# FFT filter and gated FFN: the first batch's loads as 128 rows, and the next batch's first x loads asked for earlier

## The chip, the cores and the metric

The kernel runs on one core of one Trainium2 chip. The metric is the device time of one execution in microseconds (us); the median of three runs is 1565.5 us (1564.04 to 1566.27).

## What is computed

For each of 8 batches, x (3136 positions by 256 channels) is filtered in the frequency domain along the positions, and the result goes through a feed-forward block with a gate:

```python
X = np.fft.rfft(x, axis=1)
y = np.fft.irfft(X * (filt_r + 1j * filt_i)[None], n=3136, axis=1)   # (8, 3136, 256)
h = np.maximum(y @ w_in, 0.0)                                        # 256 -> 1024
conv[s] = sum(conv_w[k] * h[s + k - 1] for k in range(3))            # zero outside the batch
out = (h * sigmoid(conv) @ w_out).astype(np.float32)                 # 1024 -> 256
```

## The kernel before

The transform of length 3136 is split as 112 x 28. A batch passes four kinds of matmul work, each in 14 pairs of columns (`NP = 14`): the first stage (112-point transforms with the tables `s1`), the second stage (28-point), a multiplication with the filter (`filt`), and the way back (third and fourth stage, the fourth with the tables `m2` or `m2g`). Its result is y, kept in SBUF as a high and a low part; the feed-forward block then reads y.

The program has an opening and a main loop. In the **opening** batch 0 is transformed alone, and nothing of the feed-forward block runs:

- Stage 1 (`first_loads`, `turned_stage` with the tile `rows`): seven pairs of loads, each one table chunk (`tab`, four columns of `s1`, 112 rows of 1792 bytes) and one chunk of x (`rows`, 112 rows of 4096 bytes). TensorE multiplies (matmuls on tile `rows`, L333), ScalarE copies the result into `at` (L385).
- Meanwhile VectorE and GpSimd turn weights from float64 words (`raw`, 512 KB for each half, loaded with 128 rows of 4096 bytes by `load_weights`; `conv_raw`, 24 KB) into float32 pairs. The generator `early` issues these steps, 35 VectorE instructions during stage 1 (L168 to L180).
- Stage 2 (the loop over `i`): TensorE transposes (L341) and multiplies by the second-stage table (L246); VectorE applies the filter in three instructions for each pair (`filt`, L261 to L263) and GpSimd adds (L264, tile `z`, three buffers); TensorE multiplies again (L333, tile `z`), ScalarE copies into `bt` (L404). Each pair needs one filter tile `f` (128 rows of 4096 bytes, four buffers, `load_filter`), asked for when VectorE has done the filter of four pairs before.
- In the same loop, at `i = 14` and `15`, TensorE does the first stage of the first two pairs of batch 1 (`AHEAD = 2`, tile `xa`, L242), stored to DRAM from ScalarE's queue. Behind each of the two stands, on TensorE, a third-stage multiplication of batch 0 that frees a `z` buffer.
- Stage 3: the way back (L343, L272), y's high part on ScalarE (L154) and low part on VectorE (L157), with further conversion steps of `early` between.

In the **main loop** the feed-forward of batch b runs with the transforms of batch b+1 between its matmuls, laid out by the table `plan`. It loads x for batch 1 as the tile `tin` (112 rows).

All loads named here are issued by SyncE's queue (SP), in one order, and the engines' orders are those of the code. A DMA issue on SP waits until the issue eight places before it has landed, because there are eight semaphores in rotation, and SP stands still for all that follows meanwhile.

Of the kernel before, what the change touches and what calls it, by code (L numbers as in the profile page):

```python
# [9 lines left out]
F32 = mybir.dt.float32  # L10
# [7 lines left out]
N1 = 112  # L18
N2 = 28
G = 28  # L20
D = 256
# [7 lines left out]
def _k1(g, s):  # L29
    return g + 1 + 28 * s  # L30


def _w(num, den):
    return np.exp(-2j * np.pi * (np.asarray(num) % den) / den)


def _dft_tables():

    n1, n2, c, a = np.arange(N1), np.arange(N2), np.arange(N2), np.arange(N1)
    n = 28 * a + c[:, None]
    s1 = np.zeros((N1, N2, 112))
    m2 = np.zeros((112, N2, N1))
    for g in range(G):
        for s in range(2):  # L50
            if g == G - 1 and s == 1:
                s1[:, :, 2 * 28 + g] = 1.0
                s1[:, :, 3 * 28 + g] = ((-1.0) ** n1)[:, None]
                m2[2 * 28 + g] = 1.0 / S
                m2[3 * 28 + g] = (-1.0) ** a / S
                continue
            k1 = _k1(g, s)
            w = _w(k1 * (28 * n1[:, None] + n2[None, :]), S)
            s1[:, :, 2 * s * 28 + g] = w.real
            s1[:, :, (2 * s + 1) * 28 + g] = w.imag  # L60
            w = np.conj(_w(k1 * n, S))
            m2[2 * s * 28 + g] = 2 * w.real / S
            m2[(2 * s + 1) * 28 + g] = -2 * w.imag / S

    def s3(special):
        m = np.zeros((2, 2, 28, N2, 4))
        for s in range(2):
            for j in range(28):
                if special and s == 1:
                    if j == 0:  # L70
                        m[0, s, 0, :, 2] = 1.0
                        m[1, s, 0, :, 2] = (-1.0) ** c
                    elif j < 14:
                        w = np.conj(_w(j * c, N2))
                        m[0, s, j, :, 2] = 2 * w.real
                        m[1, s, j, :, 2] = -2 * w.imag
                    else:
                        w = np.conj(_w((56 + 112 * (j - 14)) * c, S))
                        m[0, s, j, :, 3] = 2 * w.real
                        m[1, s, j, :, 3] = -2 * w.imag  # L80
                    continue
                k2, sg = (j, 1) if j < 14 else (41 - j, -1)
                w = np.conj(_w(k2 * c, N2))
                m[0, s, j, :, 2 * s] = w.real
                m[1, s, j, :, 2 * s] = -sg * w.imag
                m[0, s, j, :, 2 * s + 1] = w.imag
                m[1, s, j, :, 2 * s + 1] = sg * w.real
        m = m.reshape(2, 56, 112)
        return np.concatenate([m[0], np.zeros((8, 112)), m[1]])

    def s2(special):
        m = np.zeros((112, 2, 2, 28))
        for s in range(2):
            for j in range(28):
                if special and s == 1:
                    if j == 0:
                        m[n2 * 4 + 2, 0, s, 0] = 1.0
                        m[n2 * 4 + 2, 1, s, 0] = (-1.0) ** n2
                    else:
                        w = _w(n2 * j, N2) if j < 14 else _w(n2 * (56 + 112 * (j - 14)), S)  # L100
                        r = 2 if j < 14 else 3
                        m[n2 * 4 + r, 0, s, j] = w.real
                        m[n2 * 4 + r, 1, s, j] = w.imag
                    continue
                k2, sg = (j, 1) if j < 14 else (41 - j, -1)
                w = _w(n2 * k2, N2)
                m[n2 * 4 + 2 * s, 0, s, j] = w.real
                m[n2 * 4 + 2 * s + 1, 0, s, j] = -w.imag
                m[n2 * 4 + 2 * s, 1, s, j] = sg * w.imag
                m[n2 * 4 + 2 * s + 1, 1, s, j] = sg * w.real  # L110
        re, im, gap = m[:, 0].reshape(112, 56), m[:, 1].reshape(112, 56), np.zeros((112, 8))
        return np.concatenate([re, gap, im, -im, gap, re], 1)

    turned = m2.reshape(4, G, N2, N1).transpose(1, 0, 2, 3).reshape(112, N2, N1)
    return {"s1": s1, "s2": s2(False), "s2s": s2(True), "one": np.eye(128), "s3": s3(False), "s3s": s3(True), "m2": m2, "m2g": turned}


def _bins():
# [12 lines left out]
def tile_fft_filter_gated_ffn(  # L131
# [18 lines left out]
    nc = tc.nc  # L150
# [42 lines left out]
    a_in = [t[:].rearrange("n (r g) d -> (n r) g d", g=G) for t in a_dram]  # L193
    b_out = [t[:].rearrange("n (r g) d -> (n r) g d", g=G) for t in b_dram]
    b_in = [t[:].rearrange("n p d -> p n d") for t in b_dram]
    xv = [x[b].rearrange("(p n) d -> p n d", n=N2) for b in range(B)]

    wc = ctx.enter_context(tc.tile_pool(name="wc", bufs=1))
# [10 lines left out]
    turned = [wc.tile([120, 2, D], F32, name=f"v{k}") for k in range(2)]  # L209
# [15 lines left out]
    NP = 14  # L225

    def pair(q):
        return slice(2 * q, 2 * q + 2)

    def load_in(pool, kind, b, q, bufs, tag):  # L230
        r = pool.tile([112, 2, D], F32, name=tag, bufs=bufs)
        nc.sync.dma_start(out=r, in_={"1": xv, "2": a_in, "4": b_in}[kind][b][:, pair(q)])
        return r
# [46 lines left out]
    conv_raw = tp.tile([128, 1, 6 * NF], I32, name="conv_raw", bufs=1)  # L280

    def load_weights(k, pool):
        raws[k] = raw = pool.tile([128, 2, 1024], I32, name="raw", bufs=1 if pool is tp else 2)
        for part, w in enumerate((w_in, w_out)):
            nc.sync.dma_start(out=raw[:, part], in_=w[:, 1024 * k:1024 * k + 1024])
# [23 lines left out]
    with (  # L309
# [4 lines left out]
        fts, tabs, rows, zs, pss = {}, {}, {}, {}, {}  # L314
# [33 lines left out]
        with tc.tile_pool(name="sq", bufs=2) as sq:  # L348
            at = sq.tile([128, KT, N2, 112], F32, name="at", bufs=1)

            def table(kind, c):
                pool, src, n = {"1": (sq, s1, 4), "4": (sc, m2g, 3)}[kind]
                tabs[kind, c] = t = pool.tile([112, 4, 112], F32, name=f"tab{kind}", bufs=n)
                nc.sync.dma_start(out=t, in_=src[:, 4 * c:4 * c + 4])

            def tab(kind, q):
                return tabs[kind, q // 2][:, 2 * (q % 2):2 * (q % 2) + 2]
# [4 lines left out]

            def first_loads(c):
                table("1", c)
                rows["x", c] = r = sq.tile([112, 4, D], F32, name="rows", bufs=5)
                nc.sync.dma_start(out=r, in_=xv[0][:, 4 * c:4 * c + 4])
                if c == 0:
                    nc.sync.dma_start(out=conv_raw[:, 0], in_=conv_w)
                if c in (0, 3):
                    load_weights(c // 3, sc)  # L370
                if c == 4:
                    for dst, t in ((one_sb, one), (s2_sb, s2[:, 0:120]), (s2s_sb, s2s[:, 0:120]), (s3_sb, s3), (s3s_sb, s3s)):
                        nc.sync.dma_start(out=dst, in_=t)
# [16 lines left out]
            for i in range(NP + 4):  # L390
                if i < NP:
                    back = [at[:, k].rearrange("p n (r g) -> p (n r) g", g=G) for k in range(KT)]
                    rows["2", i] = turn_back(lambda j, k: back[k][:, :, 2 * i + j], sq, "ar")
                if 0 <= i - 1 < NP:
                    pss[i - 1] = ps = bank()
                    second(ps, i - 1, rows.pop(("2", i - 1)))
                if 0 <= i - NP < AHEAD:
                    ps = bank()
                    by_column(ps, tab("1", i - NP), rows.pop(("1", i - NP)))
                    store(tp, "1", 1, i - NP, ps, 3, "st", nc.scalar)  # L400
                if 0 <= i - 4 < NP:
                    q = i - 4
                    ps = turned_stage(zs.pop(q), [by_r[q == NP - 1 and j].rearrange("p r c -> p (r c)") for j in range(2)])
                    nc.scalar.activation(bt[:, :, pair(q)], ps, AF.Copy)  # L404
                if 0 <= i - 2 < NP:
                    zs[i - 2] = filt(pss.pop(i - 2), i - 2, fts.pop(i - 2))
                    if i + 2 < NP:
                        load_filter(i + 2)
                if i == NP - 3:
                    table("1", 0)  # L410
                    for q in range(AHEAD):
                        rows["1", q] = load_in(sq, "1", 1, q, 2, "xa")
                    for c in range(3):
                        table("4", c)
                    load_weights(3, tp)
                if i >= NP + 1:
                    steps(early, 3)
# [193 lines left out]
    def want_table(n):  # L611
        for op in tables[n:n + 1]:
            src = {"1": s1, "4": m2}[op[0]]
            got_table[op] = t = tp.tile([112, 2, 112], F32, name="tab", bufs=4)
            nc.sync.dma_start(out=t, in_=src[:, pair(op[2])])

    def want_filter(n):
        for op in filters[n:n + 1]:
# [133 lines left out]
```

## Time and profile before

| | |
|---|---|
| median of three runs | 1565.5 us |
| profiled execution, its own time | 1563.99 us |
| its span, first to last instruction | 1562.2 us |
| busy share of TensorE / VectorE / ScalarE / GpSimd | 98% / 76% / 73% / 53% |
| mean granted TensorE clock | 0.994 |
| chain that ended last: TensorE / DMA / ScalarE | 94% / 2% / 2% |

In the profile PE is TensorE's matmul part, PEld its weight loads, DVE VectorE, ACT ScalarE, POOL GpSimd and SP SyncE; DMA issues have the mark q behind the engine. A fp32 matmul of the program stands in the trace as two.

### The profile page before, as it was taken

The page shows a single profiled execution, that of the slowest core. Times are in us where ns is not written, and L with a number is a line of the kernel's source. Part 1 is how long each engine was busy: PE and PEld are TensorE (multiplying, and loading weights), DVE is VectorE, ACT ScalarE, POOL GpSimd, SP SyncE. Part 2 cuts the span into 40 slices and gives each one's busy share as a digit, 9 for nine tenths or more (in the row PEclk, how much of TensorE's full clock was granted, in tenths as well). Part 3 has the DMA queues.
Part 4 walks back from the last instruction along what each step waited for, and adds up shares of the span by engine and source line. Part 5 has one row for each costly group of instructions (what it writes and reads, how often), then busy time and mean ns, then how long its engine had stood idle before and what let it go on. Part 6 is the DMA issues. An engine that isn't in the chain of part 4 may idle for free.

```text
span 1562.2 us, 26445 instructions
## 1 busy us (share of the span) xinstructions
PE 1524.6 (98%) x9202; PEld 1295.2 (83%) x9202; DVE 1184.5 (76%) x1810; ACT 1144.8 (73%) x1973; POOL 828.5 (53%) x721
## 2 busy tenths in 40 slices
PE   6899999999999999999999999999999999999999
PEld 5777788877897789977898778987799878999998
DVE  6887776787677786778767777777867888777776
ACT  2486678866797668866688667976678667888886
POOL 4535446544474555744566444745457454664444
PEclk9999999999999999999999999999999999999999
DMA  9857764466436654465554655356542543300000
GB/s 261 260 164 202 208 180 138 138 196 192 145 91 200 193 156 142 120 198 179 153 150 129 198 178 162 109 161 208 169 143 86 160 150 96 114 28 15 28 28 30
DMA packets 158164, 228.74 MB, mean 146 GB/s; under 512 B 16432, under 2 KB 108960, under 8 KB 158032
## 3 DMA queue, kind: packets, MB, share of 16 engines
q1 hardware_dynamic: 157552, 226.60, 48.9%
q8 instruction: 73, 1.20, 0.3%
q14 instruction: 59, 0.48, 0.1%
q10 hardware_dynamic: 480, 0.46, 0.1%
HBM read 156.35 MB, written 70.65 MB: 145 GB/s over the span
## 4 chain that ended last, share of the span: by engine, by line
PE 94%; DMA 2%; ACT 2%; issue 1%; SPq 0%; DVE 0%; POOL 0%; ACTq 0%; POOLq 0%
PE ps_h L185 12%; PE ps_h L186 12%; PE ps_h L187 12%; PE po L528 11%; PE po L530 11%; PE po L529 11%; PE ps_t L246 10%; PE ps_t L272 6%; PE ps_t L242 5%; PE ps L333 1%; DMA rows<-in_x 1%; PE ps_t L249 1%; PE ps L246 1%; PE ps L341 1%; PE ps L272 1%
## 5 line engine op out<-in xcount | busy, mean ns | idle before, releaser
L496 DVE SCALAR_TENSOR_TENSOR t<-ps_h,cw,t 128x510 f32<-128x510 f32 (+1 forms) x800 | 588.1, 735 | 302.1 <-ACT t L492 298.9
L160 POOL TENSOR_TENSOR g<-t,g 128x510 fp32r<-128x510 f32 (+1 forms) x400 | 506.0, 1274 | 203.4 <-ACT g L154 191.7
L528 PE MATMUL po<-wo,g 128*128 128x256 f32 (+1 forms) x1576 | 439.9, 279 | 0.1
L530 PE MATMUL po<-wo,g 128*128 128x256 f32 (+1 forms) x1576 | 439.1, 279 | 0.0
L529 PE MATMUL po<-wo,g 128*128 128x256 f32 (+1 forms) x1576 | 438.9, 278 | 0.0
L487 ACT ACTIVATE ps_h<-ps_h 128x512 f32<-128x512 f32 (+1 forms) x400 | 234.8, 587 | 243.0 <-PE ps_h L187 241.5
L264 POOL TENSOR_TENSOR z<-z,v 120x512 f32<-120x512 f32 x112 | 144.6, 1291 | 389.5 <-DVE v L263 337.9
L492 ACT ACTIVATE t<-ps_h,cw 128x510 f32<-128x510 f32 (+1 forms) x400 | 272.6, 682 | 104.2 <-POOL g L160 71.6
L185 PE MATMUL ps_h<-y,wi 128*128 128x512 f32 (+1 forms) x688 | 333.3, 484 | 0.5 <-DVE y L157 0.5
L528 PEld LDWEIGHTS po<-wo,g 128*128 128x128 f32 (+1 forms) x1576 | 296.9, 188 | 17.4 <-ACT g L154 0.3
L529 PEld LDWEIGHTS po<-wo,g 128*128 128x128 f32 (+1 forms) x1576 | 296.1, 188 | 17.0
L530 PEld LDWEIGHTS po<-wo,g 128*128 128x128 f32 (+1 forms) x1576 | 296.4, 188 | 0.6 <-POOL g L160 0.5
L186 PE MATMUL ps_h<-y,wi 128*128 128x512 f32 (+1 forms) x688 | 270.1, 393 | 0.0
L187 PE MATMUL ps_h<-y,wi 128*128 128x512 f32 (+1 forms) x688 | 269.9, 392 | 0.0
L502 DVE TENSOR_TENSOR t<-ps_h,t 128x510 f32<-128x510 f32 (+1 forms) x400 | 268.3, 671 | 0.9 <-ACT t L499 0.8
L499 ACT ACTIVATE t<-t 128x510 f32<-128x510 f32 (+1 forms) x400 | 245.2, 613 | 1.6 <-DVE t L496 1.5
L154 ACT ACTIVATE g<-t 128x510 fp32r<-128x510 f32 (+1 forms) x400 | 245.0, 613 | 0.2 <-DVE t L502 0.2
L160 POOL TENSOR_TENSOR y<-z,y 128x448 fp32r<-128x448 f32 x98 | 138.5, 1423 | 93.9 <-ACT y L154 91.9
L185 PEld LDWEIGHTS ps_h<-y,wi 128*128 128x128 f32 x688 | 130.2, 189 | 44.2 <-issue 23.8
L186 PEld LDWEIGHTS ps_h<-y,wi 128*128 128x128 f32 x688 | 130.5, 190 | 41.4 <-issue 24.3
L187 PEld LDWEIGHTS ps_h<-y,wi 128*128 128x128 f32 x688 | 130.0, 189 | 30.3 <-POOL wi L160 0.2
L237 ACT ACTIVATE st<-ps_t 112x512 f32<-112x512 f32 x194 | 114.1, 591 | 11.3 <-PE ps_t L242 11.0
(91 smaller groups left out, 1616.0 us busy)
## 6 DMA issues: line engine op xcount, KB each, us to landing
filt<-in_filt SPq DMA_DIRECT2D x98, 512.0 KB
tin<-a_dram SPq DMA_DIRECT2D x98, 224.0 KB
b_dram<-st SPq DMA_DIRECT2D x98, 224.0 KB
tin<-b_dram SPq DMA_DIRECT2D x98, 224.0 KB
tin<-in_x SPq DMA_DIRECT2D x96, 224.0 KB
a_dram<-st SPq DMA_DIRECT2D x96, 224.0 KB
out<-ot SPq DMA_DIRECT2D x45, 256.0 KB
tab<-in_m SPq DMA_DIRECT2D x98, 98.0 KB
```

The source lines that it names most:

```text
L154: nc.scalar.activation(dst, src, AF.Copy)
L160: nc.gpsimd.tensor_tensor(out=dst, in0=src, in1=hi.bitcast(F32), op=ALU.subtract)
L185: nc.tensor.matmul(ps, lhsT=wh, rhs=rh, start=start, stop=False, **kw)
L186: nc.tensor.matmul(ps, lhsT=wh, rhs=rl, start=False, stop=False, **kw)
L187: nc.tensor.matmul(ps, lhsT=wl, rhs=rh, start=False, stop=stop, **kw)
L492: nc.scalar.activation(t, hs[u, f][:, 1:n + 1], AF.Copy, scale=cw[:, 1, f:f + 1])
L496: nc.vector.scalar_tensor_tensor(out=t, in0=h[:, k:place(u)[2] + k], scalar=cw[:, k, f:f + 1], in1=t, op0=ALU.mult, op1=ALU.add)
L499: nc.scalar.activation(ts[u, f], ts[u, f], AF.Sigmoid)
L502: nc.vector.tensor_mul(ts[u, f], hs.pop((u, f))[:, 1:place(u)[2] + 1], ts[u, f])
L528: nc.tensor.matmul(o, lhsT=gh[:, c:c + n], rhs=wo[0][:, f], start=first, stop=False, skip_group_check=True)
L529: nc.tensor.matmul(o, lhsT=gh[:, c:c + n], rhs=wo[1][:, f], start=False, stop=False, skip_group_check=True)
L530: nc.tensor.matmul(o, lhsT=gl[:, c:c + n], rhs=wo[0][:, f], start=False, stop=last, skip_group_check=True)
```

## The change

Three things. The first-stage tables get 16 rows of zeros, so that the table chunk and the chunk of x of each pair in stage 1 are loaded as 128 rows; the last 16 rows of x are the first ones of batch 1, and the computation reads rows 0 to 111. The load of `conv_raw` goes from ahead of the first weights to behind the second pair. The two `xa` loads and their table, asked for at `i = 11` before, are asked for at `i = 5`, and `xa` too is loaded as 128 rows.

```diff
+    tall = np.zeros((128, N2, 112))
+    tall[:N1] = s1
-    return {"s1": s1, ...
+    return {"s1": tall, ...
...
+    xt = x.rearrange("b (p n) d -> (b p) n d", n=N2)
...
             def table(kind, c):
                 pool, src, n = {"1": (sq, s1, 4), "4": (sc, m2g, 3)}[kind]
-                tabs[kind, c] = t = pool.tile([112, 4, 112], F32, name=f"tab{kind}", bufs=n)
+                t = pool.tile([src.shape[0], 4, 112], F32, name=f"tab{kind}", bufs=n)
                 nc.sync.dma_start(out=t, in_=src[:, 4 * c:4 * c + 4])
+                tabs[kind, c] = t[0:112]
...
             def first_loads(c):
                 table("1", c)
-                rows["x", c] = r = sq.tile([112, 4, D], F32, name="rows", bufs=5)
-                nc.sync.dma_start(out=r, in_=xv[0][:, 4 * c:4 * c + 4])
-                if c == 0:
-                    nc.sync.dma_start(out=conv_raw[:, 0], in_=conv_w)
+                r = sq.tile([128, 4, D], F32, name="rows", bufs=5)
+                nc.sync.dma_start(out=r, in_=xt[0:128, 4 * c:4 * c + 4])
+                rows["x", c] = r[0:112]
                 if c in (0, 3):
                     load_weights(c // 3, sc)
+                if c == 1:
+                    nc.sync.dma_start(out=conv_raw[:, 0], in_=conv_w)
...
-                if i == NP - 3:
+                if i == 5:
                     table("1", 0)
                     for q in range(AHEAD):
-                        rows["1", q] = load_in(sq, "1", 1, q, 2, "xa")
+                        r = sq.tile([128, 2, D], F32, name="xa", bufs=2)
+                        nc.sync.dma_start(out=r, in_=xt[N1:N1 + 128, pair(q)])
+                        rows["1", q] = r[0:112]
+                if i == NP - 3:
                     for c in range(3):
                         table("4", c)
```

Only SP's order changes. At the program's start it stood so before (`tab` with `in_s` is a table chunk, `rows` the chunk of x, `raw` the weights):

```order
L354 DMA tab_111<-in_s 112x448
L366 DMA rows<-in_x 112x1024
L368 DMA conv_raw<-in_conv_w 128x48
L285 DMA raw<-in_w_in 128x1024
L285 DMA raw<-in_w_out 128x1024
L354 DMA tab_119<-in_s 112x448
L366 DMA rows<-in_x 112x1024
```

And now:

```order
L357 DMA tab_111<-in_s 128x448
L370 DMA rows<-in_x 128x1024
L288 DMA raw<-in_w_in 128x1024
L288 DMA raw<-in_w_out 128x1024
L357 DMA tab_118<-in_s 128x448
L370 DMA rows<-in_x 128x1024
L375 DMA conv_raw<-in_conv_w 128x48
```

The pairs carry 128 rows, and the 24 KB of `conv_raw` stand three places later, behind the first weights and the second pair.

In stage 2, SP's order among the filter loads `f` was this before, with three of the main loop's x loads (`tin`) between them:

```order
L361 DMA f<-in_filt 128x1024 x4
L232 DMA tin<-in_x 112x512
L361 DMA f<-in_filt 128x1024 x2
L232 DMA tin<-in_x 112x512
L361 DMA f<-in_filt 128x1024 x2
L232 DMA tin<-in_x 112x512
L361 DMA f<-in_filt 128x1024 x2
L354 DMA tab_532<-in_s 112x448
L232 DMA xa<-in_x 112x512 x2
L354 DMA tab_538<-in_m2g 112x448
```

And now:

```order
L365 DMA f<-in_filt 128x1024 x4
L357 DMA tab_400<-in_s 128x448
L418 DMA xa<-in_x 128x512 x2
L365 DMA f<-in_filt 128x1024 x6
L357 DMA tab_538<-in_m2g 112x448
L357 DMA tab_540<-in_m2g 112x448
L357 DMA tab_542<-in_m2g 112x448
L288 DMA raw<-in_w_in 128x1024
L288 DMA raw<-in_w_out 128x1024
L235 DMA tin<-in_x 112x512 x5
```

`xa` and its table moved ahead of the last six filter loads; and the scheduler, which the code does not tell so, put all five early `tin` loads behind them, where three stood among the filter loads and two behind the last weights before.

More of the change, by code (lines that the diff above doesn't have):

```diff
@@ L114, in _dft_tables @@
     turned = m2.reshape(4, G, N2, N1).transpose(1, 0, 2, 3).reshape(112, N2, N1)
-    return {"s1": s1, "s2": s2(False), "s2s": s2(True), "one": np.eye(128), "s3": s3(False), "s3s": s3(True), "m2": m2, "m2g": turned}
+    tall = np.zeros((128, N2, 112))
+    tall[:N1] = s1
+    return {"s1": tall, "s2": s2(False), "s2s": s2(True), "one": np.eye(128), "s3": s3(False), "s3s": s3(True), "m2": m2, "m2g": turned}
 def _bins():
@@ L614, in want_table @@
             got_table[op] = t = tp.tile([112, 2, 112], F32, name="tab", bufs=4)
-            nc.sync.dma_start(out=t, in_=src[:, pair(op[2])])
+            nc.sync.dma_start(out=t, in_=src[0:112, pair(op[2])])
     def want_filter(n):
```

## Prediction

> **What bounds the kernel now.** I read the page first, then the chain that ended last cut to its first 100 us, then the waits, the order of time on SP, VectorE and ScalarE, and stretches. The page says that TensorE is the bound of the program as a whole:
>
> ```profile
> PE 1524.6 (98%) x9202; PEld 1295.2 (83%) x9202; DVE 1184.5 (76%) x1810; ACT 1144.8 (73%) x1973; POOL 828.5 (53%) x721
> ```
>
> The change touches none of TensorE's work, so it can act only where TensorE isn't the bound. The chain up to 100 us (start, length, what) shows where that is:
>
> ```profile
> 3.55 8.56 DMA rows<-in_x
> 12.12 11.45 DMA rows<-in_x
> 27.45 5.61 PE ps L333 x32
> 58.63 6.88 DMA xa<-in_x
> ...
> 96.31 0.99 DVE y L157
> ```
>
> Up to 23.6 us the chain is loads of x, and at 58.6 us it is the load of `xa`. The waits of the opening (us in total, times, longest) name who stands still for them:
>
> ```profile
> DVE em L168 <- DMA raw<-in_w_out: 9.9, 1, 9.9
> PE ps L333 <- DMA rows<-in_x: 11.9, 3, 5.5
> DVE z L261 <- PE ps L246: 3.4, 1, 3.4
> PE ps L242 <- DMA xa<-in_x: 4.2, 1, 4.2
> DVE z L261 <- PE ps L333: 5.1, 1, 5.1
> ```
>
> TensorE waits three times for x, VectorE once for the first weights. From about 97.4 us, when the first feed-forward matmul starts, every engine's work is the same in both programs and nothing in it depends on absolute time. So the gain is how much earlier the opening ends.
>
> **Who bounds the opening.** Busy time of VectorE, the third figure after the length, in its three parts (PE, PEld, DVE, ACT, POOL, clock, DMA share, GB/s):
>
> ```profile
> 9.86:32.80 22.94, 16.58 (x96) 16.22 (x96) 22.01 (x35) 5.99 (x11) 13.99 (x18) 0.85 1.04 279
> 36.22:64.27 28.05, 25.22 (x156) 18.84 (x154) 26.91 (x39) 12.20 (x22) 15.32 (x12) 1.00 0.83 242
> 69.38:97.44 28.06, 26.48 (x205) 24.71 (x204) 27.35 (x33) 23.12 (x35) 14.19 (x28) 0.95 0.35 99
> ```
>
> VectorE is busy for 22.0 of 22.9 us, 26.9 of 28.1 and 27.4 of 28.1. Between lie two gaps, 32.8 to 36.2 and 64.3 to 69.4. The opening is then a sum: first weights landed (9.86), 22.94 of conversion, a gap of 3.42, thirteen filter steps of 2.16 (28.05), a gap of 5.11, and 28.06 to the first matmul of the feed-forward.
>
> ```profile
> 9.86 0.43 DVE L168 TENSOR_SCALAR em<-raw 128x512 int32<-128x512 int32 x1 [9.86 <-DMA raw<-in_w_out]
> 32.05 0.75 DVE L180 SCALAR_TENSOR_TENSOR em<-raw,em 128x512 f32<-128x512 uint32 x1
> 36.22 0.69 DVE L261 TENSOR_TENSOR z<-ps,f 120x512 f32<-120x512 f32 x1 [3.42 <-PE ps L246]
> 62.11 0.69 DVE L261 TENSOR_TENSOR z<-ps,f 120x512 f32<-120x512 f32 x1
> 69.38 0.69 DVE L261 TENSOR_TENSOR z<-ps,f 120x512 f32<-120x512 f32 x1 [5.14 <-PE ps L333]
> ```
>
> The change can take from the first term and from the two gaps. The other three are instructions that it leaves as they are.
>
> **Part 1, 128 rows.** The rate of loads of different kinds, from stretches with the same columns:
>
> ```profile
> 10.00:13.00 3.00, 0.76 (x4) 0.79 (x4) 2.86 (x6) 0.00 (x0) 0.00 (x0) 1.00 1.06 257
> 20.00:23.00 3.00, 0.37 (x4) 0.19 (x2) 2.79 (x5) 0.60 (x2) 2.94 (x5) 1.00 1.06 223
> 31.00:36.00 5.00, 4.12 (x27) 3.27 (x27) 1.73 (x3) 2.72 (x5) 2.05 (x3) 0.98 1.01 401
> ```
>
> In all three the DMA engines are full (share 1.0). From 31 to 36 us only filter tiles and weights move, 128 rows of 4 KB: 401 GB/s. From 10 to 13 it is mostly table chunks and x with 112 rows: 257. That a chunk of x alone, also of 4 KB rows, is slow shows on SP, whose issue waits for the landing eight places before; the times are thus landings:
>
> ```profile
> 12.12 0.33 SPq L366 DMA_DIRECT2D rows<-in_x  x1
> 12.91 0.35 SPq L373 DMA_DIRECT2D one_sb<-in_one  x1
> 14.71 0.31 SPq L373 DMA_DIRECT2D s_sb<-in_s  x1
> 15.51 0.31 SPq L373 DMA_DIRECT2D s2s_sb<-in_s2s  x1
> 17.72 0.36 SPq L373 DMA_DIRECT2D s_sb<-in_s  x1
> 23.64 0.31 SPq L354 DMA_DIRECT2D tab<-in_s  x1
> ```
>
> 12.12 is the landing of the second x chunk, 12.91 of a table, 14.71 of x, 15.51 table, 17.72 x, 23.64 the fifth x. A chunk of x (459 KB) takes 1.80 and 2.21 us after its table, 255 and 208 GB/s; a table (201 KB) 0.8 us. From 12.12 to 23.64 three pairs of 660 KB and 1.05 MB of weights land; the weights at 401 GB/s are 2.6 us, which leaves 8.9, or 2.97 a pair.
>
> With 128 rows a pair is 754 KB. At 401 GB/s it takes 1.88 us, 1.09 less. If only x speeds up (524 KB, 1.31 us) and the table stays at 0.8 us for its first 112 rows (0.9 for 128), it takes 2.2, 0.76 less. The rows of 1.8 KB haven't been seen with 128, so I keep both ends and take 0.9. Six pairs lie ahead of the restart at 27.45, which waits for the sixth chunk: 4.6 to 6.5 us earlier, 5.4 taken. From there ScalarE's last copy of stage 1 ended 6.2 us later:
>
> ```profile
> 33.08 0.55 ACT L385 ACTIVATE at<-ps 128x448 f32<-128x448 f32 x1 [0.35 <-PE ps L333]
> ```
>
> That is 33.63, and the first filter step came 2.59 us after it. Moved by 5.4 us, TensorE has the first filter step ready at 36.22 - 5.4 = 30.8 (29.7 to 31.6).
>
> **But VectorE** must first have converted. Its start hangs on the first weights, behind one pair: 1.76 MB landed by 9.86 before, 1.80 MB now.
>
> ```profile
> 0.74 0.40 SPq L354 DMA_DIRECT2D tab<-in_s  x1
> 5.48 3.73 PE L333 MATMUL ps<-tab,rows 112*128 112x112 f32 x16 [5.48 <-DMA rows<-in_x]
> ```
>
> The first pair (0.66 MB) was there 4.74 us after the first issue; 1.6 to 2.6 us of that is moving it, at 401 or 257 GB/s, so 2.1 to 3.1 is start and completion. With it, 1.80 MB at 401 GB/s (4.5 us) are there at 7.3 to 8.3. I take 7.9, 2.0 us earlier, and 22.94 later VectorE is free at 30.8. Both ends meet there. The later of the two sets the step: 31.0 taken, 30.3 to 31.6, a gain of **5.2 us** (4.6 to 5.9). What has been waited for 3.42 us in the gap is thus almost used up, and behind it VectorE is the limit: faster loads still would bring nothing.
>
> **Part 2, `conv_raw` later.** 24 KB less ahead of the weights, inside the estimate above. It is needed after fourteen conversion steps, at 19.47 before, and lands with the second pair, before 12 us: nothing.
>
> **Part 3, `xa` earlier.** The wait at 69.38 stands under a product of the third stage (L333). In TensorE's order this product is behind the `xa` product; it frees the `z` buffer that VectorE's last filter step writes, three buffers back. SP's rows:
>
> ```profile
> 55.62 2.49 SPq L361 DMA_DIRECT2D f<-in_filt  x2
> 58.63 0.89 SPq L232 DMA_DIRECT2D xa<-in_x  x2
> 61.41 0.35 SPq L285 DMA_DIRECT2D raw<-in_w_in  x1
> 64.71 0.35 SPq L285 DMA_DIRECT2D raw<-in_w_out  x1
> 65.65 2.02 PE L242 MATMUL ps<-xa,tab 112*112 112x256 f32 x4 [4.21 <-DMA xa<-in_x]
> ```
>
> `xa` was asked for at 58.63 and used at 65.65. Now it is asked for behind four filter loads, that is after the fourth filter step: 31.0 + 4 x 2.16 = 39.7, and used at about 65.65 - 4.2 - 5.2 = 56. Even the 7 us of before leave 9 to spare. The last step would then follow its forerunner: 64.27 instead of 69.38, **5.1 us** less. The two `xa` products themselves (2.02 us at half clock, now without the idle time that lowered it) come between, where TensorE has dropped its transposes.
>
> What it puts in others' way: 753 KB ahead of the ninth filter tile, 1.9 us at 401 GB/s or 2.9 at 257. A filter tile is asked for three steps, 6.5 us, ahead of its use and needs 1.3 us to move and 2.1 to 3.1 around it: 5.3 to 7.3. That is hidden but for 0.8 us at worst, 0 taken. For it the three `tin` loads are gone from there, among which the last filter tile had landed only by 64.71, the issue it released: without that, `xa` alone would have brought 4.7. The five `tin` loads and the last weights come after the thirteenth filter tile, from 53 us on; what is then queued, 4 MB, is 14 us at 282 GB/s, and the loop starts near 87: hidden.
>
> **The sum.** 5.2 + 5.1 = 10.3 us, against the profiled execution 1563.99 - 10.3 = 1553.7; the median shown stands 1.5 above it, so 1565.5 - 10.3 = **1555.2**. Its own range by the bounds is 8.9 (4.6 + 5.1 - 0.8) to 11.0 (5.9 + 5.1) less, 1554.5 to 1556.6, with 1 us of spread between runs 1553.5 to 1557.6.
>
> **Rivals.** About 0.2%, 3.1 us, is what can be told from no change.
>
> *128 rows bring nothing in stage 1 (10 in 100).* Row count may not be what made x slow. If time per pair stays, only `xa` counts: 1565.5 - 5.1 = 1560.4. If the byte rate stays, each pair costs 0.42 more (2.97 x 16/112), six pairs 2.5, net 2.6: 1562.9. Against it speaks that x and filter rows have the same 4 KB.
>
> The Trainium skill, "SBUF — State Buffer", section "Door 1: The DMA port swizzle", gives each of 16 ports eight partitions, and by its table the busiest port still has eight with 112 rows; "DMA: Bandwidth & Descriptors", "Why a DMA increments its semaphore by 16 and not by 1", picks the largest divisor up to 16 of the row count, 16 for both. By these two alone a pair would take as long as before, and the sum would be 1560.4. The trace (208 to 257 against 401 GB/s) doesn't agree with such an equality, so it keeps a small chance.
>
> *The wait moves to the filter tiles (5 in 100).* If the ninth and later tiles come late behind `xa` by as much as it waited, part 3 gives nothing: 1565.5 - 5.2 = 1560.3.
>
> *The main loop takes it back (5 in 100).* All five `tin` loads are now behind the last weights. If they came only 10 us after the loop could start, the gain would be gone: 1565.5. The 14 us of queue above would have to be 44.
>
> *Slower (4 in 100).* The 128-row loads, whose last rows belong to another batch, could be slow themselves. With part 3 saved, the opening gets 3.1 us longer if the sixth chunk comes 8.2 later, 1.37 a pair: 4.34 us for 754 KB. So below 174 GB/s it is slower; at 150 GB/s a pair is 5.0 us, six pairs 12.3 more, and the time 1565.5 + 12.3 - 5.1 = 1572.7. The lowest full stretch above is 223.
>
> **The numbers.** The forecast has 76 in 100. Faster by over 0.2%: 76, 5 of the second rival and 7 of the first's 10, 0.88. Within 0.2%: 3 and 5, 0.08. Slower: 0.04. The range goes from 1553.0, the forecast's fast end with half a us more, to 1560.8, which takes in the two rivals with 5 us.
>
> **What would show it.** In the profile after: VectorE's first conversion at 7.3 to 8.3; x landing on SP every 1.9 to 2.2 us; a first filter step near 31, straight after the last conversion; no wait for `xa`; filter steps 2.16 apart to the last, near 59; the first feed-forward matmul near 87. Wrong would make it: pairs still 3 us apart, a filter step waiting for `f`, or TensorE starved for `tin` behind 87 us.

## The result, and the profile after

The changed kernel takes 1556.05 us (median of four runs, 1554.59 to 1557.19) against 1564.77 for the kernel before, ratio 0.9950 with a 95% interval of 0.9938 to 0.9963. That is 8.7 us less; 1555.2 had been forecast, 10.3 less than the 1565.5 known then. Its profiled execution took 1554.59 us, with a span of 1552.8. Runs on other chips are compared below with the kernel before on the same chip.

The page and the first 100 us of the chain that ended last:

```profile
span 1552.8 us, 26446 instructions
PE 1519.7 (98%) x9202; PEld 1290.6 (83%) x9202; DVE 1185.3 (76%) x1810; ACT 1144.7 (74%) x1973; POOL 828.3 (53%) x721
3.08 7.69 DMA rows<-in_x
11.22 7.18 DMA rows<-in_x
...
42.41 6.61 DMA f<-in_filt
...
87.73 0.99 DVE y L159
```

The loads of x are still in the chain, but up to 18.4 us and not 23.6. The link at 18.4 is the profile's guess: the VectorE step there reads `conv_raw`, which had landed before 11.2, and VectorE had not stood idle ahead of it. From there on up to stage 2 the chain is VectorE's conversions, which began at 8.79. The `xa` load is gone from the chain; a load of a filter tile `f` at 42.4 has come in. VectorE's terms of the opening, in the order of time:

```profile
8.79 0.43 DVE L170 TENSOR_SCALAR em<-raw 128x512 int32<-128x512 int32 x1 [8.79 <-DMA raw<-in_w_out]
31.01 0.76 DVE L182 SCALAR_TENSOR_TENSOR em<-raw,em 128x512 f32<-128x512 uint32 x1
31.69 0.68 DVE L264 TENSOR_TENSOR z<-ps,f 120x512 f32<-120x512 f32 x1
49.12 0.69 DVE L264 TENSOR_TENSOR z<-ps,f 120x512 f32<-120x512 f32 x1 [0.24 <-DMA f<-in_filt]
57.76 0.69 DVE L264 TENSOR_TENSOR z<-ps,f 120x512 f32<-120x512 f32 x1
59.92 0.69 DVE L264 TENSOR_TENSOR z<-ps,f 120x512 f32<-120x512 f32 x1
```

The first filter step follows straight on the last conversion, and the last one comes 2.16 us behind its forerunner, the distance at which steps follow without a wait: both gaps are closed. The ninth step, at 49.12, waits 0.24 us for its filter tile. The opening ends with the first feed-forward matmul, in the kernel before and in the changed one:

```profile
97.44 0.47 PE L185 MATMUL ps_h<-y,wi 128*128 128x512 f32 x1 [0.48 <-DVE y L157]
88.85 0.47 PE L187 MATMUL ps_h<-y,wi 128*128 128x512 f32 x1 [0.50 <-DVE y L159]
```

| us | before | after | difference |
|---|---|---|---|
| first conversion | 9.86 | 8.79 | -1.07 |
| from there to the first filter step | 26.36 | 22.90 | -3.46 |
| first to last filter step | 33.16 | 28.23 | -4.93 |
| last filter step to the first feed-forward matmul | 28.06 | 28.93 | +0.87 |
| from there to the end of the span | 1464.76 | 1463.95 | -0.81 |

The landings of the second to the fifth chunk of x, by the issues on SP that they release:

```profile
10.85 0.33 SPq L357 DMA_DIRECT2D tab<-in_s  x1
12.75 0.34 SPq L378 DMA_DIRECT2D s_sb<-in_s  x1
14.63 0.38 SPq L378 DMA_DIRECT2D s_sb<-in_s  x1
19.56 0.33 SPq L357 DMA_DIRECT2D tab<-in_s  x1
```

10.85, 12.75, 14.63: 1.90 and 1.88 us a pair. Stretches of the same trace (the last three figures are TensorE's granted clock, the DMA share and GB/s):

```profile
10.00:13.00 3.00, 2.09 (x10) 2.12 (x11) 2.86 (x7) 0.04 (x1) 0.19 (x1) 1.00 1.04 413
13.00:18.00 5.00, 5.00 (x39) 5.00 (x39) 4.83 (x6) 2.68 (x5) 4.41 (x5) 1.00 1.03 405
65.50:69.50 4.00, 4.00 (x20) 3.75 (x21) 3.86 (x7) 1.60 (x3) 3.37 (x5) 0.57 1.03 302
2.00:8.00 6.00, 2.82 (x13) 2.85 (x14) 0.00 (x0) 0.76 (x3) 0.00 (x0) 1.00 0.94 317
```

With 128 rows the stretch at 10 to 13 us runs at 413 GB/s, where it ran at 257. The third row shows something new: TensorE's clock is near half when stage 3 begins. The fourth shows that the first loads, also of 128 rows, moved at only 317 GB/s, at a share of 0.94.

### The profile page after: what moved, and what is told of

Read it like the earlier page. It is cut to its first block, busy times and chain, and to the rows that moved or that the text cites. A ratio compares the mean times of both kernels' runs of the same rounds, so it can differ in the third digit from the quotient of the medians.

```text
span 1552.8 us, 26446 instructions
## 1 busy us (share of the span) xinstructions
PE 1519.7 (98%) x9202; PEld 1290.6 (83%) x9202; DVE 1185.3 (76%) x1810; ACT 1144.7 (74%) x1973; POOL 828.3 (53%) x721
## 4 chain that ended last, share of the span: by engine, by line
PE 92%; DVE 2%; ACT 2%; DMA 2%; issue 2%; SPq 0%; POOL 0%; ACTq 0%; POOLq 0%; DVEq 0%
PE ps_h L187 12%; PE ps_h L189 12%; PE ps_h L188 12%; PE po L536 12%; PE po L538 12%; PE po L537 11%; PE ps_t L249 10%; PE ps_t L275 6%; PE ps_t L245 5%; DMA rows<-in_x 1%; PE ps_t L252 1%; ACT br L346 0%; DVE v L265 0%; DVE z L264 0%; DMA f<-in_filt 0%
## 5 line engine op out<-in xcount | busy, mean ns | idle before, releaser
L187 PEld LDWEIGHTS ps_h<-y,wi 128*128 128x128 f32 x688 | 130.4, 189 | 44.3 <-issue 23.6
L240 ACT ACTIVATE st<-ps_t 112x512 f32<-112x512 f32 x194 | 114.0, 590 | 11.2 <-PE ps_t L245 11.1
```

What stands on the lines that cost most here:

```text
L187: nc.tensor.matmul(ps, lhsT=wh, rhs=rh, start=start, stop=False, **kw)
```

## The experiments

### The two parts apart

The 128 rows of stage 1 alone, with `conv_raw` and `xa` as before:

```diff
+                if c == 0:
+                    nc.sync.dma_start(out=conv_raw[:, 0], in_=conv_w)
...
-                if c == 1:
-                    nc.sync.dma_start(out=conv_raw[:, 0], in_=conv_w)
...
-                if i == 5:
+                if i == NP - 3:
                     table("1", 0)
                     for q in range(AHEAD):
-                        r = sq.tile([128, 2, D], F32, name="xa", bufs=2)
...
+                        rows["1", q] = load_in(sq, "1", 1, q, 2, "xa")
```

> Only the 128 rows of stage 1; conv_raw and xa stand where they stood before. Theory (the terms add): the first filter step at 31.7 to 32.1 us, the wait of about 5 us in front of the last filter step stays, the last filter step at 64.9, the first feed-forward matmul 4.5 us earlier than before, at 92.9; time 4.5 us less. Rival (the two parts share one cause, a queue of loads that the faster stage 1 empties): the wait for xa goes too, the first feed-forward matmul at 88 to 89, time 8.6 less.

`xa` alone, in the kernel before:

```diff
-                if i == NP - 3:
+                if i == 5:
                     table("1", 0)
                     for q in range(AHEAD):
                         rows["1", q] = load_in(sq, "1", 1, q, 2, "xa")
+                if i == NP - 3:
                     for c in range(3):
```

> Only xa and its table asked for at i = 5, with 112 rows; stage 1 and conv_raw as before. Theory (the terms add): the first filter step at 36.2, steps 2.16 apart to the last at 64.3 to 64.7, the first feed-forward matmul 4 to 5 us earlier than before, at 92.5 to 93.4 (the upper end if TensorE's clock falls to half ahead of stage 3 as in the changed kernel). Time 4.1 to 4.9 less. Rival (xa gains only when stage 1 is faster, the filter tiles come late instead): waits for f of 3 us or more, the first feed-forward matmul at 96 or later.

Ratios to before on one chip: 0.9976 (0.9964 to 0.9989) with the rows alone, 0.9982 (0.9971 to 0.9992) with `xa` alone. Added up they make 0.9958, inside the interval of the changed kernel (0.9938 to 0.9963). The last filter step with the rows alone, and that with `xa` alone:

```profile
65.03 0.69 DVE L264 TENSOR_TENSOR z<-ps,f 120x512 f32<-120x512 f32 x1 [4.62 <-PE ps L336]
65.44 0.69 DVE L261 TENSOR_TENSOR z<-ps,f 120x512 f32<-120x512 f32 x1
```

With the rows alone the first filter step came at 31.78 and the wait ahead of the last stayed at 4.62; the first feed-forward matmul came at 93.12, 4.3 earlier, as the theory had it. The eighth and the ninth filter step waited 0.32 and 0.38 us for their tiles there, although `xa` stood behind all the filter loads. With `xa` alone the wait was gone, but the matmul came at 95.28, only 2.2 earlier and outside what was expected. Two things took 2.8 us back:

```profile
54.63 0.69 DVE L261 TENSOR_TENSOR z<-ps,f 120x512 f32<-120x512 f32 x1 [1.06 <-PE ps L341]
69.00:76.00 7.00, 6.16 (x29) 5.63 (x30) 6.83 (x8) 2.08 (x4) 6.24 (x8) 0.54 1.05 314
```

The ninth filter step is 1.06 late. The profile names transposes of TensorE, but the step reads nothing of theirs; in the other kernels a filter tile is named at this place, so a late tile is the likely cause. And the clock was half for almost all of 69 to 76 us; from the last filter step to the feed-forward 29.84 us passed, 1.78 more than before. So in these profiles the half clock comes with moving `xa`, with or without the faster rows. The late tile comes in part with the faster rows alone (0.70 us above).

### Is the half clock the 0.9 us of stage 3?

In the changed kernel TensorE waits three times up to the first products of stage 3 (L344), for the last two z on GpSimd and for ScalarE's copy:

```profile
61.39 1.15 PE L336 MATMUL ps<-by_r,z 120*128 120x112 f32 x8 [0.97 <-POOL z L267]
63.69 1.15 PE L336 MATMUL ps<-by_r,z 120*128 120x112 f32 x8 [1.16 <-POOL z L267]
65.47 1.70 PE L344 MATMUL ps<-one_sb,bt 128*112 128x128 f32 x8 [0.63 <-ACT bt L409]
```

The changed kernel, with the `xa` products on TensorE at `i = 16` and `17`:

```diff
-                if 0 <= i - NP < AHEAD:
+                if 0 <= i - NP - 2 < AHEAD:
                     ps = bank()
-                    by_column(ps, tab("1", i - NP), rows.pop(("1", i - NP)))
-                    store(tp, "1", 1, i - NP, ps, 3, "st", nc.scalar)
+                    by_column(ps, tab("1", i - NP - 2), rows.pop(("1", i - NP - 2)))
+                    store(tp, "1", 1, i - NP - 2, ps, 3, "st", nc.scalar)
```

> The changed kernel with the two xa products two steps later in the loop (i = 16 and 17), where TensorE otherwise waits for the last two z. Theory (the 0.9 us that stage 3 is longer comes from TensorE's clock falling to half between 65.5 and 69.5): the clock stays full, ScalarE's first y about 1 us earlier, the first feed-forward matmul at 87.9 to 88.1 instead of 88.85; time 0.8 less. Rival (it comes from the loads that now lie ahead of stage 3): clock full or not, the first feed-forward matmul stays at 88.7 to 89.

```profile
61.06 0.69 DVE L264 TENSOR_TENSOR z<-ps,f 120x512 f32<-120x512 f32 x1
61.00:68.50 7.50, 6.17 (x41) 4.80 (x40) 7.24 (x10) 3.91 (x7) 6.34 (x6) 1.00 1.05 319
89.13 0.47 PE L187 MATMUL ps_h<-y,wi 128*128 128x512 f32 x1 [0.49 <-DVE y L159]
```

The clock stayed full, and the stretch from the last filter step to the feed-forward took 28.07 us instead of 28.93: 0.86 back, the size expected. ScalarE's first y came 8.12 us behind the last filter step instead of 9.17. The matmul itself came later than expected, at 89.13, because the ninth filter tile was 1.33 us late in this execution. The loads were the same, so the rival falls for stage 3. Ratio to before 0.9943 (0.9923 to 0.9962); by time alone it isn't apart from the changed kernel.

The profiles of the other kernels, among them those of the sections below, show the same:

| profiled executions | last filter step to the feed-forward, us | mean granted clock there |
|---|---|---|
| `xa` products late | 28.07 | 1.00 |
| x back at 112 rows | 28.06 | 1.00 |
| changed kernel twice, first weights ahead, tables at 112 rows | 28.90 to 28.93 | 0.94 |
| `xa` alone, 120 rows, `conv_raw` back twice | 29.84 to 30.15 | 0.89 |
| the last two kernels below, `xa` products late, with another wait behind stage 3 | 28.67 and 28.80 | 1.00 |

The kernel with x back at 112 rows has the `xa` products early, and nearly the same waits as the changed kernel, 0.96, 1.16 and 0.63 us; the last two:

```profile
72.03 1.15 PE L336 MATMUL ps<-by_r,z 120*128 120x112 f32 x8 [1.16 <-POOL z L267]
73.81 1.13 PE L344 MATMUL ps<-one_sb,bt 128*112 128x128 f32 x8 [0.63 <-ACT bt L408]
```

Yet its clock stayed full, and the stretch took 28.06 us. So it is the clock that lengthens the stretch, and these waits don't always lower it: they did in eight of nine executions with early products, and in none of three with late ones.

### What bounds the first filter step?

The changed kernel, with the first weights asked for ahead of the first pair:

```diff
             def first_loads(c):
+                if c == 0:
+                    load_weights(0, sc)
                 table("1", c)
...
-                if c in (0, 3):
-                    load_weights(c // 3, sc)
+                if c == 3:
+                    load_weights(1, sc)
```

> The changed kernel with the first weights asked for ahead of the first pair. Theory (VectorE's start is the bound of the first filter step): first conversion at 6.6 to 6.9 instead of 8.8, TensorE's first product at 7.5 to 8.2 instead of 5.2, the first filter step at 29.6 to 30.2 instead of 31.7, the first feed-forward matmul at 86.8 to 87.3; time 1.6 to 2.0 less than the changed kernel. Rival (x bounds it after all): TensorE's end of stage 1 moves back by the 2.6 us by which x comes later, the first filter step at 32 or later, time the same or up to 1 us more.

```profile
6.06 0.43 DVE L170 TENSOR_SCALAR em<-raw 128x512 int32<-128x512 int32 x1 [6.06 <-DMA raw<-in_w_out]
29.64 0.69 DVE L264 TENSOR_TENSOR z<-ps,f 120x512 f32<-120x512 f32 x1 [0.60 <-PE ps L249]
48.52 0.69 DVE L264 TENSOR_TENSOR z<-ps,f 120x512 f32<-120x512 f32 x1 [1.03 <-DMA f<-in_filt]
88.23 0.47 PE L187 MATMUL ps_h<-y,wi 128*128 128x512 f32 x1 [0.49 <-DVE y L159]
```

The first filter step came 2.05 us earlier, at 29.64, though x came later: VectorE's start was the bound, and now TensorE is, by 0.6. The rest was lost again: the eighth and ninth filter step waited 0.68 and 1.03 us, and the first feed-forward matmul was only 0.6 earlier than in the changed kernel, later than the 86.8 to 87.3 expected. For the eighth step the profile names a product of TensorE, for the ninth a filter tile. Ratio to before 0.9941 (0.9923 to 0.9959), not apart from the changed kernel.

### Why 128 rows are faster

Four kernels change only the loads of stage 1, each from the changed kernel. One run of each stands on a chip on which the kernel before took 1562.0 us. Tables back at 112 rows:

```diff
-                t = pool.tile([src.shape[0], 4, 112], F32, name=f"tab{kind}", bufs=n)
-                nc.sync.dma_start(out=t, in_=src[:, 4 * c:4 * c + 4])
+                t = pool.tile([112, 4, 112], F32, name=f"tab{kind}", bufs=n)
+                nc.sync.dma_start(out=t, in_=src[0:112, 4 * c:4 * c + 4])
```

> The changed kernel with the tables back at 112 rows, x at 128. Theory (row count makes the rate, for rows of 1.8 and of 4 KB alike; a mixture gains in part, by its share of bytes): about 30% of a pair's bytes stay slow, x land on SP 2.2 us apart instead of 1.9, the end of stage 1 on ScalarE 1 to 2.5 us later than 27.0. Rival A (any load of 112 rows sets the 16 engines out of step, and the loads behind it suffer): stage 1 ends 4 us or more later, near the 33.6 of before. Rival B (only x matters): 27.0 as in the changed kernel.

x back at 112 rows:

```diff
-                r = sq.tile([128, 4, D], F32, name="rows", bufs=5)
-                nc.sync.dma_start(out=r, in_=xt[0:128, 4 * c:4 * c + 4])
-                rows["x", c] = r[0:112]
+                rows["x", c] = r = sq.tile([112, 4, D], F32, name="rows", bufs=5)
+                nc.sync.dma_start(out=r, in_=xv[0][:, 4 * c:4 * c + 4])
```

> The changed kernel with x back at 112 rows, the tables at 128. Theory (share of bytes): 70% of a pair's bytes stay slow, stage 1 ends 4 to 5.5 us later than 27.0, at 31 to 32.5. Rival A (any load of 112 rows spoils all): 33 to 34. Rival B (the short rows of the tables were what was slow): 27 to 29.

120 rows for both:

```diff
-    tall = np.zeros((128, N2, 112))
+    tall = np.zeros((120, N2, 112))
...
-                r = sq.tile([128, 4, D], F32, name="rows", bufs=5)
-                nc.sync.dma_start(out=r, in_=xt[0:128, 4 * c:4 * c + 4])
+                r = sq.tile([120, 4, D], F32, name="rows", bufs=5)
+                nc.sync.dma_start(out=r, in_=xt[0:120, 4 * c:4 * c + 4])
```

> The changed kernel with 120 rows in place of 128 in x and tables of stage 1. Theory (a rule of the Trainium skill, DMA: Bandwidth & Descriptors: a load runs on the largest number of engines up to 16 that divides its row count; 120 rows would run on 15, eight rows on each): rates of about 15/16 of 400 if eight rows on each engine are what counts, 375 GB/s, x 2.0 us apart, stage 1 ends at 27 to 28. Rival (only all 128 partitions give each engine its own port; any other count collides): rates near 260 as with 112 rows, stage 1 ends at 32 or later.

ScalarE's last copy of stage 1 in the changed kernel, with 112 rows in the tables, in x, and 120 in both:

```profile
26.44 0.54 ACT L390 ACTIVATE at<-ps 128x448 f32<-128x448 f32 x1 [0.35 <-PE ps L336]
28.45 0.55 ACT L390 ACTIVATE at<-ps 128x448 f32<-128x448 f32 x1 [0.35 <-PE ps L336]
34.32 0.54 ACT L389 ACTIVATE at<-ps 128x448 f32<-128x448 f32 x1 [1.16 <-PE ps L336]
34.95 0.54 ACT L390 ACTIVATE at<-ps 128x448 f32<-128x448 f32 x1 [0.68 <-PE ps L336]
```

And the rates with 120 rows:

```profile
10.00:13.00 3.00, 0.61 (x4) 0.62 (x4) 2.83 (x6) 0.54 (x1) 0.00 (x0) 1.00 1.05 260
24.00:31.00 7.00, 6.47 (x29) 6.26 (x30) 6.72 (x11) 1.64 (x3) 4.31 (x5) 0.50 1.02 259
```

120 rows are as slow as 112: 260 and 259 GB/s, and the time of that run, 1562.8 us, is that of the kernel before. So it isn't the bytes; of the row counts tried only 128 is fast. The 375 GB/s that eight rows on each of fifteen engines were to give did not come, so that estimate fails. That the ports collide is the rival's reading; no row here shows a port, and why 128 is fast stays open.

The single times are 1555.3 us with the tables at 112 rows and 1560.9 with x at 112. With x at 128 and the tables at 112 stage 1 ends 2.0 us later, as the share of bytes had it. The other way round it ends at 34.9, later than all three had it and nearest to rival A. But TensorE's clock was half there for the last pairs, as it was before the change (0.50 from 25 to 31 us), which adds to both. The loads alone show in TensorE's restart with the sixth chunk of x, in the changed kernel, with the tables at 112 and with x at 112:

```profile
22.55 3.85 PE L336 MATMUL ps<-tab,rows 112*128 112x112 f32 x32 [0.91 <-DMA rows<-in_x]
24.53 3.89 PE L336 MATMUL ps<-tab,rows 112*128 112x112 f32 x32 [1.66 <-DMA rows<-in_x]
27.68 6.61 PE L336 MATMUL ps<-tab,rows 112*128 112x112 f32 x32 [1.93 <-DMA rows<-in_x]
```

The last two pairs took 6.61 us instead of 3.85, so 2.8 of the 7.9 us by which stage 1 ends late with x at 112 are the clock. The sixth chunk itself came 2.0 and 5.1 us late; before the change it came at 27.45, 4.9 late. Tables with 128 rows between chunks of x with 112 bring nothing, and x alone brings three fifths. By the share of bytes it would have been 1.5 and 3.4 late, so a share of bytes doesn't explain both kernels.

The fourth kernel has `conv_raw` back:

```diff
+                if c == 0:
+                    nc.sync.dma_start(out=conv_raw[:, 0], in_=conv_w)
...
-                if c == 1:
-                    nc.sync.dma_start(out=conv_raw[:, 0], in_=conv_w)
```

> The changed kernel with conv_raw back ahead of the first weights. Theory (24 KB cost nothing of note): first conversion at 8.8 to 8.9 us, first filter step at 31.7 to 31.8, as in the kernel with the 128 rows alone, which has conv_raw there too and began at 8.88. Rival (its rows of 192 bytes are slow and hold up the weights): first conversion at 9.2 or later.

The first conversion came at 8.96, but the last chunk of x came late, TensorE waited 1.72 us for it and went to half clock, and the first filter step was at 33.66. The kernel with the rows alone, with the same loads in the same order up to there, had shown nothing of it. The kernel with `conv_raw` back was run a second time, timed:

> The kernel with conv_raw back in its old place once more, timed. In its first profile the seventh chunk of x came 1.7 us late, TensorE's clock fell to half at 26.7 us and the first filter step came at 33.7. The kernel with the 128 rows alone issues the same loads in the same order up to there and showed none of it. Theory (chance of one execution): ratio to before 0.9945 as for the changed kernel (0.9930 to 0.9962), first filter step at 31.7 to 32.5 in this profile. Rival (conv_raw ahead of the weights makes the last chunk late): ratio 0.9965 or more, the late chunk and the half clock again, first filter step at 33 or later.

```profile
33.66 0.69 DVE L264 TENSOR_TENSOR z<-ps,f 120x512 f32<-120x512 f32 x1 [1.72 <-PE ps L249]
32.31 0.68 DVE L264 TENSOR_TENSOR z<-ps,f 120x512 f32<-120x512 f32 x1
```

The second execution has its first filter step at 32.31, 22.9 behind its first conversion, and the ratio is 0.9954 (0.9942 to 0.9966), beside 0.9945 (0.9929 to 0.9962) for the changed kernel run again. The late chunk did not come again in the second profile. A cost of `conv_raw` ahead isn't shown.

### The three losses together, and the main loop

The changed kernel was run again beside the next two:

> The changed kernel once more, on one chip with the next two. Every theory expects what it showed: first conversion 8.8 us, first filter step 31.7, last 59.9, first feed-forward matmul 88.9, 8.6 earlier than before. What may differ is the wait for the ninth filter tile: in the changed kernel and in the three kernels with xa asked for at i = 5 it was 0.2 to 1.7 us (with the step beside it); expected here 0.2 to 1.3, which moves the last steps as much.

```profile
50.94 0.69 DVE L264 TENSOR_TENSOR z<-ps,f 120x512 f32<-120x512 f32 x1 [1.09 <-DMA f<-in_filt]
90.67 0.47 PE L187 MATMUL ps_h<-y,wi 128*128 128x512 f32 x1 [0.49 <-DVE y L159]
```

Here the weights landed at 9.52 and filter tiles were 1.35 us late in all, so the opening took 1.8 us longer than in its first profile: one execution's opening can differ from another's by that much. The median was 1554.8 us, against 1562.85 before.

First weights ahead, `xa` products late as above, and `xa` asked for behind the third weights:

```diff
                 if q == 8:
                     for k in range(4):
                         load_filter(k)
                     load_weights(2, sc)
+                    table("1", 0)
+                    for k in range(AHEAD):
+                        r = sq.tile([128, 2, D], F32, name="xa", bufs=2)
+                        nc.sync.dma_start(out=r, in_=xt[N1:N1 + 128, pair(k)])
+                        rows["1", k] = r[0:112]
...
-                if i == 5:
...
```

> The changed kernel with the first weights ahead of the first pair, xa and its table asked for behind the third weights (at 23 us, where the queue runs empty at 31), and the xa products at i = 16 and 17. Theory (three separate losses: VectorE's start, the ninth filter tile behind 753 KB of xa, the half clock ahead of stage 3): first filter step 29.6, no wait for f, last filter step 57.7 to 57.9, clock full up to stage 3, first feed-forward matmul 85.8 to 86.0, 3.0 us earlier than the changed kernel; time about 3 less. Rival (the filter tiles are late because stage 2 asks for them too late at 243 GB/s, whatever lies between): a wait for f stays, 1 us or more, first feed-forward matmul 86.8 or later.

```profile
57.71 0.69 DVE L264 TENSOR_TENSOR z<-ps,f 120x512 f32<-120x512 f32 x1 [0.43 <-DMA f<-in_filt]
85.74 1.12 PE L245 MATMUL ps_t<-tin,tab 112*112 112x256 f32 x4 [1.26 <-DVE y L159]
86.51 0.58 PE L187 MATMUL ps_h<-y,wi 128*128 128x512 f32 x1
```

The first filter step was at 29.26, no step waited at the ninth filter tile, and the last was at 57.71. A wait of 0.43 for the last tile is left; the scheduler now put two `tin` loads among the last filter loads. The first feed-forward matmul came at 86.51, 0.5 to 0.7 later than expected: behind stage 3 a product of the loop now waits 1.26 us for VectorE's y, which the changed kernel does not show. Median 1552.15, ratio to before 0.9930 (0.9915 to 0.9945), against 0.9945 for the changed kernel on the same chip; the profile shows 2.3 us less opening than the changed kernel's first execution and 4.2 less than its second, but the intervals overlap.

That kernel with the loop's loads of x for batches 1 to 6 as 128 rows as well:

```diff
+        wide = kind == "1" and b < B - 1
-        r = pool.tile([112, 2, D], F32, name=tag, bufs=bufs)
-        nc.sync.dma_start(out=r, in_={"1": xv, "2": a_in, "4": b_in}[kind][b][:, pair(q)])
-        return r
+        r = pool.tile([128, 2, D], F32, name=tag, bufs=bufs)
+        if wide:
+            nc.sync.dma_start(out=r, in_=xt[N1 * b:N1 * b + 128, pair(q)])
+        else:
+            nc.sync.dma_start(out=r[0:112], in_={"1": xv, "2": a_in, "4": b_in}[kind][b][:, pair(q)])
+        return r[0:112]
```

> The kernel of the run before, and in the main loop the 82 loads of x for batches 1 to 6 also as 128 rows (batch 7 has no rows behind it). Theory (128 rows bring time only where an engine waits for loads): the opening as in the run before, the main loop the same within 1 us, since TensorE's waits for loads in its first 28 us come to 1.4 us in all; time 0 to 1.4 less. Rival (the main loop's first part, with the DMA engines full at 250 to 320 GB/s, is limited by the 112 rows): the first 28 us of the loop shorter by 1.5 us or more.

```profile
55.78 0.69 DVE L268 TENSOR_TENSOR z<-ps,f 120x512 f32<-120x512 f32 x1 [0.40 <-DMA f<-in_filt]
59.19 0.69 DVE L268 TENSOR_TENSOR z<-ps,f 120x512 f32<-120x512 f32 x1 [1.28 <-DMA f<-in_filt]
```

In this execution two of the last filter steps waited for their tiles, 1.7 us in all, and the first feed-forward matmul came at 87.86. So late filter tiles stay even with `xa` out of their way; they have moved to the last ones. From the first feed-forward matmul to the first product with `po` it took 22.25 us, against 22.21 without these rows and 22.09 in the changed kernel: the loop's first part gained nothing. Median 1551.42, ratio 0.9925 (0.9910 to 0.9940), the lowest of all; its own gain over the kernel without is 0.7 us between medians, inside their spread.

## Why the prediction was right, point by point

- **The gain is how much earlier the opening ends.** Held: 8.59 of the 9.4 us between the spans lie there. The forecast was 10.3, with 8.9 to 11.0 by its own bounds, so the opening gained a little less than these allowed. The 1.7 us that are missing are 0.7 at the first filter step, 0.2 between the filter steps and 0.9 behind the last. The other 0.8 are in the loop; over the profiles shown whose loop is unchanged it took from 1461.0 to 1464.8 us, so they aren't explained, and needn't be of this change. That they bring this pair of profiles nearer to the forecast is luck.
- **128 rows at 401 GB/s, 1.88 us a pair.** Held: 1.88 and 1.90. That the tables of 1.8 KB rows speed up too was the end taken only in part; between 10 and 18 us 405 to 413 GB/s were reached. The sixth chunk released TensorE at 22.55 instead of 27.45, 4.9 earlier, inside the 4.6 to 6.5. The 6.2 us from there to the end of stage 1 did not stay, as the working had it, but became 4.4: the clock, half there before, was now full.
- **First weights at 7.9, 2.0 us earlier.** Mis-sized: 8.79, 1.07 earlier. The step put 1.80 MB at 401 GB/s behind 2.1 to 3.1 us of start. From 2 to 8 us the loads ran at 317 GB/s, at a share of 0.94, and in six other profiles with 128 rows at 316 to 349; an average of over 400 came only from 10 us on. At 317 GB/s the 1.80 MB take 5.7 us instead of 4.5. Because the first filter step hangs on it, that came at 31.69 instead of 31.0. (The 1.76 MB named for the kernel before add up to 1.73.)
- **VectorE sets the first filter step, the gap of 3.42 is used up, faster loads bring nothing more.** Held: the step at 31.69 follows the last conversion, and moving the weights moved it by 2.05.
- **`conv_raw` nothing.** No cost was shown.
- **`xa` removes 5.1 us.** Held for the wait itself. Its side cost, "0.8 us at worst, 0 taken" for the ninth filter tile, was too small: 0.24 in the first profile of the changed kernel, but 1.35 at the eighth and ninth step together in its second, and 1.1 to 1.9 in the eight other executions with `xa` at `i = 5`. The bound of 5.3 to 7.3 us for a tile was too low: the ninth was asked for at 42.41 in the changed kernel's first profile and used at 49.12, 6.7 us later, but in the nine others it took 7.5 to 8.4. Moving `xa` is only part of it: with the rows alone the ninth tile took 7.1 us, with one `tin` load and no `xa` ahead of it. Why it differs so between executions stays open.
- **The last 28.06 us stay.** Mis-sized by 0.87. The two `xa` products were said to run without the idle time that lowered the clock, and they do. But in the kernel before they came so late, behind the wait for `xa`, that TensorE worked from 65.7 to 74.3 us without a pause, and its clock was full again when stage 3 began, at 74.95 (the rows below, of the kernel before). Now they are done early, TensorE waits for the last two z, and the clock falls as stage 3 begins.

```profile
69.14 1.91 PE L242 MATMUL ps<-xa,tab 112*112 112x256 f32 x4
70.84 3.48 PE L333 MATMUL ps<-by_r,z 120*128 120x112 f32 x24
74.95 1.13 PE L341 MATMUL ps<-one_sb,bt 128*112 128x128 f32 x8 [0.64 <-ACT bt L404]
```

- **The loop's `tin` loads hidden.** Held: the loop's first part took 22.07 us to the first `po` product before and 22.09 after.
- **The rivals.** None came about. The second was there in small, 0.2 to 1.9 us of its 5.1. The first, equal time a pair, was read out of two pages of the Trainium skill together ("SBUF — State Buffer", section "Door 1: The DMA port swizzle", and "DMA: Bandwidth & Descriptors", section "Why a DMA increments its semaphore by 16 and not by 1"). This case's trace does not agree: 1.9 against 2.97 us.

## What to carry to other kernels

Split the stage into what bounds it link by link: here VectorE's path had a late start and two gaps of 3.4 and 5.1 us, and closing a gap brought only what the next link left over. Where a stage waits for loads of fewer than 128 rows, padding to 128 can gain more than its bytes cost; where loads are hidden, as in the loop here, no gain showed. A load moved earlier takes its place in a queue whose other users have a deadline, and work moved out of an engine's idle stretch can let its clock fall.

## What the runs showed of the hardware that had not been expected

- Loads of 120 rows ran at 260 GB/s like those of 112, beside 401 to 413 with 128, at the same full share of the DMA engines.
- The two kinds of load don't share the gain by their bytes. In one execution each, the sixth chunk of x released TensorE at 27.7 us with 128 rows in the tables alone, 27.5 with 112 in both, 24.5 with 128 in x alone, and 22.6 with 128 in both.
- The first loads of the program were slower than the same loads later: 317 GB/s from 2 to 8 us, 413 from 10 to 13, at shares of 0.94 and 1.04.
- TensorE's granted clock fell to 0.5 at the start of stage 3 or up to 3 us before it, in eight of nine executions with waits of up to 1, 1.2 and 0.6 us within about 5 us, and stayed there for 3 to 7 us; with products in these waits it stayed at 1.0, in three of three. The end of the opening came 0.8 to 2.1 us later with the half clock than with the full one.
